# An attention and feed-forward kernel: VectorE and ScalarE in a fixed instruction order, with an explicit list for the opening

## The chip, the cores and the metric

The kernel runs on one core of a Trainium2 chip. Five engines have instruction streams of their own: TensorE (PE; its weight loads are shown apart as PEld), VectorE (DVE), ScalarE (ACT), GpSimd (POOL) and SyncE (SP, which here only issues DMAs). The metric is the device time of one execution in microseconds, lower is better.

## The reference

For four batches of 12480 tokens with 128 features: 32 learned vectors attend to the tokens, which gives `h` (32 x 128 per batch); then every token attends to `h`; the result goes through a feed-forward network (FFN) with 2048 hidden features and the ELU function.

```python
def mab(q, kv):
    s = scale * (q @ kv.transpose(0, 2, 1))
    s = s - s.max(-1, keepdims=True)
    a = np.exp(s)
    a /= a.sum(-1, keepdims=True) + 1e-09
    return a @ kv
h = mab(I, x)                 # I: the 32 vectors, for each batch
y = mab(x, h)                 # 4 x 12480 x 128
hidden = y.reshape(-1, 128) @ w_in
g = np.where(hidden > 0.0, hidden, np.exp(np.minimum(hidden, 0.0)) - 1.0)
out = g @ w_out               # 49920 x 128, float32
```

The two weight matrices arrive as 64-bit floats and are turned into 32-bit ones on the chip, from their integer halves.

## The kernel before

**Tiling.** A batch is cut into 25 blocks (15 of 512 tokens, 10 of 480), and the blocks into seven groups of two to four (`GROUPING`). `HALVES` are the pairs of blocks in a group. A *unit* (also called a pair, since it covers two chunks of 128 hidden features) is one block times one of eight pairs of chunks: 4 x 25 x 8 = 800 units, numbered n.

**The main pipeline**, one unit at a time:

- `ffn_in` (L552): two matmuls into a PSUM tile `ph`. The projection of `h` by `w_in` is multiplied directly by the attention weights, so the second attention product and the first FFN product are one matmul (L558). ACT takes the exponential, `e` (L566). There are three `ph` slots.
- `ffn_mid` (L569): DVE combines `ph` and `e` into ELU plus one (L572), into `ph` for units marked D, else into `e`.
- `ffn_split` (L576): the value is split into a high part `gh` (ACT, L581) and a low part `gl`. For D units DVE makes `gl` from `ph` (L584); for P units POOL does, in two steps (L589, L594); N units need only POOL's first step, and use plain 32-bit matmuls. `PLAN = "PDNPDPND"` gives the mark of each of a block's eight units.
- `ffn_out` (L596): matmuls (L616) of `gh`, `gl` or `e` with parts of `w_out` into an accumulator `po`, five units behind `ffn_in`; after the eighth unit DVE transposes the block (L623) and SP stores it.

**Side work.** While the FFN of batch b runs, its attention is prepared group by group (`attend`: scores L483 on PE and a DVE transpose L491; maximum L499, subtraction L500, exponential L503; sum, reciprocal and product L510 to L513; a transpose L521, a split L530 and L531, and DMAs into the six `stk` tiles L536). In the same time batch b+1 goes through its first attention (`first_half`: `load_xT` with a DMA and a DVE transpose L239, `scores` L284, `bias_of`, `weights_of` L345, `e_of` L358, `gather` L361, and the chain from `sum_es` to `stack_h` that ends in the tile `hw`). Each side step has a due time in blocks, written as a formula; the loop at L751 emits a step when its due time has come.

**What sets the order.** A planner in the framework orders each engine's instructions from its own model of their times. From the first unit on, only PE is held to the program's order (`tc.manual_schedule(engines={ET.PE})`); the transposes L239 and, after the opening, the exponentials L345 are held behind the instruction that precedes them on their engine. All other work on DVE, ACT, POOL and SP is placed by the planner. Small PSUM results of side steps use one of the two `po` slots (`bank`).

**The opening.** `first_batch` (L674) does the first half for batch 0: PE transposes of `x`, copies, scores in two phases (groups 0 to 2, then 3 to 6; `PHASES`), and the conversion of the weights in 16 pieces of 256 columns (class `Weight`, L145). The attention of block 0 alone (`attend(0, -1)`) and the projection of `h` by `w_in` end it. The planner orders all engines here.

Of the kernel before, what the change touches and what calls it, by code (L numbers as in the profile page):

```python
# [27 lines left out]
PLAN = "PDNPDPND"  # L28


@with_exitstack
def kernel(
# [47 lines left out]
    PHASES = [range(0, 3), range(3, NG)]  # L80

# [17 lines left out]

    turn = [0]  # L100

    def bank(name, take=False):
# [23 lines left out]
    ind = const.tile([M, C], F32, name="ind")  # L126
# [12 lines left out]
    WS = 256  # L139
# [5 lines left out]
    class Weight:  # L145


        def __init__(self, raw):

            self.raw = raw.rearrange("p (f two) -> p f two", two=2)  # L150

        def take_apart(self):
            lo, hi = self.raw[:, :, 0], self.raw[:, :, 1]
            part = op.tile([P, 2, WS], U32, tag="o", name="w_part")
            scale, sign = part[:, 0], part[:, 1]
            nc.vector.tensor_scalar(
                out=scale, in0=hi, scalar1=20, scalar2=0x7FF,
                op0=ALU.logical_shift_right, op1=ALU.bitwise_and,
            )
            nc.scalar.activation(sign.bitcast(F32), hi.bitcast(I32), AF.Sign)  # L160
            nc.scalar.activation(lo.bitcast(F32), lo, AF.Copy, scale=2.0**-52)
# [4 lines left out]
            nc.vector.tensor_scalar(  # L166
                out=hi, in0=hi, scalar1=0xFFFFF, scalar2=0x100000,
                op0=ALU.bitwise_and, op1=ALU.bitwise_or,
            )
            nc.gpsimd.tensor_scalar(  # L170
                out=scale, in0=scale.bitcast(F32), scalar1=-254.0, scalar2=-float(1 << 23),
                op0=ALU.add, op1=ALU.mult,
            )
            self.scale, self.low, self.top = scale.bitcast(F32), lo.bitcast(F32), hi
            self.sign = sign.bitcast(F32)

        def put_together(self, dst):
            nc.gpsimd.tensor_tensor(out=self.sign, in0=self.sign, in1=self.scale, op=ALU.mult)
            nc.vector.scalar_tensor_tensor(
                out=self.low, in0=self.top, scalar=2.0**-20, in1=self.low,  # L180
                op0=ALU.mult, op1=ALU.add,
            )
            nc.gpsimd.tensor_tensor(out=dst, in0=self.low, in1=self.sign, op=ALU.mult)
# [7 lines left out]
    def finish_w_in(s, w):  # L191
        w.put_together(win_sb[:, s * WS : (s + 1) * WS])

    WC = WS // C

    def load_w_out(quarter, pool, tag):
        n = NFC // 4
        raw = pool.tile([P, n, 2 * C], U32, tag=tag, name="w_raw")
        rows = w_out[quarter * n * P : (quarter + 1) * n * P, :]
        dma = nc.sync.dma_start(raw, rows.rearrange("(c p) d -> p c d", p=P))  # L200
        raw = raw.rearrange("p c d -> p (c d)")
        return [Weight(raw[:, i : i + 2 * WS]) for i in range(0, 2 * n * C, 2 * WS)], dma

    def finish_w_out(s, w):
        t = small.tile([P, WC, C], F32, tag="wo", name=f"wo_{s}")
        w.put_together(t.rearrange("p c d -> p (c d)"))
        for i in range(WC):
            f = s * WC + i
            if f in WHERE_N:
                nc.scalar.copy(wo_n[:, WHERE_N[f], :], t[:, i, :])  # L210
            if f in WHERE_S:
                n = WHERE_S[f]
                nc.scalar.copy(wo_h[:, n, :], t[:, i, :])
                nc.gpsimd.tensor_sub(
                    wo_l[:, n, :], t[:, i, :], wo_h[:, n, :].bitcast(F32)
                )
# [4 lines left out]
    steady = []  # L221

    def in_order(ins):
        return tc.keep_in_program_order(ins) if steady else ins

    def load_xT(b, h):
# [12 lines left out]
        tc.keep_in_program_order(nc.vector.transpose(t, xq.rearrange("p u d -> p (u d)")))  # L239
        xT[b, h] = t  # L240

    def transpose_first(b, g):
# [9 lines left out]
        for v in range(0, U, UP):  # L252
            n = min(UP, U - v)
            ps = ps_h.tile([P, 2, 512], F32, tag="ph", name=f"ps_x_{g}_{v}")
# [10 lines left out]
            for i, half in enumerate(halves):  # L265
                m = min(2, nq - 2 * i)
                copy = nc.scalar.copy if i % 2 else nc.vector.tensor_copy
# [16 lines left out]
    def scores(b, g):  # L284
# [5 lines left out]
        for j in range(nq):  # L290
# [6 lines left out]
            )  # L297

# [4 lines left out]
        )  # L303
        nc.vector.tensor_reduce(
            out=st["pm"][:np_, g : g + 1], in_=s, axis=AX.X, op=ALU.max
        )
        st["s", g] = s

    def bias_of(b, i):
        st = state[b]
        n = PHASES[i].stop
# [8 lines left out]
        nc.tensor.matmul(ps[:, : 4 * n], nsel4, apart[:, :, :n], start=True, stop=True)  # L322
        bias = small.tile([P, 1], F32, tag=f"bias{i}", name=f"bias_{b}_{i}")
        nc.vector.tensor_reduce(out=bias, in_=ps[:, : 4 * n], axis=AX.X, op=ALU.min)  # L324
        st["bias", i] = bias
        if i:
            st["scale"] = small.tile([P, 1], F32, tag="scale", name=f"scale_{b}")
            nc.scalar.activation(st["scale"], st["bias", 0], AF.Exp, bias=bias, scale=-1.0)
# [12 lines left out]
    def weights_of(b, g):  # L341
# [3 lines left out]
        in_order(nc.scalar.activation(  # L345
# [3 lines left out]
            bias=st["bias", int(g in PHASES[1])][:np_],  # L349
            scale=SCALE,  # L350
            accum_out=st["es"][:np_, g : g + 1],
        ))
# [8 lines left out]
    def gather(b, g):  # L361
        st = state[b]
        np_, U = GROUPS[g][1] * Q, GROUPS[g][2] // Q
        ps = bank(f"ps_hh_{b}_{g}")
        for u in range(U):
# [7 lines left out]
            )  # L373
        if g == 0:
            st["h"] = small.tile([P, C], F32, tag="h", name=f"h_{b}")
            nc.vector.tensor_copy(st["h"], ps[:, :C])
        elif g == PHASES[1].start:
# [420 lines left out]
```

## Time and profile before

| | |
|---|---|
| median of 3 runs | 1726.87 us (1726.18 to 1726.93) |
| the profiled execution | 1726.07 us, of it span from first to last instruction 1724.2 us |
| busy share of the span | PE 96%, DVE 89%, ACT 81%, POOL 78% |
| granted TensorE clock | mean 0.986; 0.50 from 40 to 70 us |
| first FFN matmul (L558) | at 67.6 us |
| batches 1, 2, 3 begin at | 492.4, 910.4, 1328.3 us |

A row of grouped instructions gives line, engine, operation, output and inputs with their shapes and the count, then busy microseconds and the mean in ns of one, then the engine's idle time just before them and what ended it. A row of a stretch gives its bounds and length, then busy microseconds and the number of instructions of PE, PEld, DVE, ACT and POOL, then the granted clock, the DMA share and GB/s. A row of waits gives who waited for whom, the microseconds in total, the number of times and the longest. A row of the timeline gives start, duration, engine and instruction, and in brackets the idle time before it and who ended that.

### The profile page before, as it was taken

The page shows a single profiled execution, that of the slowest core. Times are in us where ns is not written, and L with a number is a line of the kernel's source. Part 1 is how long each engine was busy: PE and PEld are TensorE (multiplying, and loading weights), DVE is VectorE, ACT ScalarE, POOL GpSimd, SP SyncE. Part 2 cuts the span into 40 slices and gives each one's busy share as a digit, 9 for nine tenths or more (in the row PEclk, how much of TensorE's full clock was granted, in tenths as well). Part 3 has the DMA queues.
Part 4 walks back from the last instruction along what each step waited for, and adds up shares of the span by engine and source line. Part 5 has one row for each costly group of instructions (what it writes and reads, how often), then busy time and mean ns, then how long its engine had stood idle before and what let it go on. Part 6 is the DMA issues. An engine that isn't in the chain of part 4 may idle for free.

```text
span 1724.2 us, 22399 instructions
## 1 busy us (share of the span) xinstructions
PE 1653.8 (96%) x7446; PEld 1174.2 (68%) x7446; DVE 1530.5 (89%) x1618; ACT 1404.2 (81%) x1643; POOL 1346.6 (78%) x970
## 2 busy tenths in 40 slices
PE   6689999999999999999999999999999999999998
PEld 4356766677676666667776676676777777777776
DVE  6889889989899998898889989888989999989986
ACT  6778888788788878888888788788878888888886
POOL 3877777778787877777778777777868888888886
PEclk9599999999999999999999999999999999999999
DMA  7363333322234233232323423411212211121111
GB/s 254 62 97 51 59 63 59 66 48 61 59 53 76 50 75 64 52 54 47 83 49 55 73 61 50 79 37 35 73 31 47 37 33 27 23 37 32 26 19 21
DMA packets 384755, 98.10 MB, mean 57 GB/s; under 512 B 364864, under 2 KB 370784, under 8 KB 384384
## 3 DMA queue, kind: packets, MB, share of 16 engines
q1 hardware_dynamic: 384640, 96.68, 29.0%
q8 instruction: 59, 0.97, 0.3%
q14 instruction: 56, 0.46, 0.1%
HBM read 48.94 MB, written 25.56 MB: 43 GB/s over the span
## 4 chain that ended last, share of the span: by engine, by line
PE 79%; DVE 10%; issue 3%; ACT 2%; DMA 1%; POOL 1%; SPq 0%; DVEq 0%; ACTq 0%; POOLq 0%
PE po L616 56%; PE ph L558 19%; DVE e L572 3%; DVE xT L239 2%; DVE gl L584 2%; ACT e L566 1%; PE ps_t L483 1%; PE ps_hh L367 1%; DVE ph L572 1%; PE ps_s L291 1%; DVE o L623 1%; DMA xq<-in_x_dram 1%; ACT gh L581 0%; ACT s L300 0%; POOL gl L594 0%
## 5 line engine op out<-in xcount | busy, mean ns | idle before, releaser
L566 ACT ACTIVATE e<-ph 128x1024 f32<-128x1024 f32 (+1 forms) x800 | 803.6, 1005 | 233.5 <-PE ph L558 227.6
L589 POOL TENSOR_SCALAR e<-e 128x1024 f32<-128x1024 f32 (+1 forms) x500 | 512.2, 1031 | 306.1 <-ACT gh L581 285.0
L594 POOL TENSOR_TENSOR gl<-e,gh 128x1024 fp32r<-128x1024 f32 (+1 forms) x300 | 704.3, 2348 | 16.6
L572 DVE SCALAR_TENSOR_TENSOR e<-ph,e 128x1024 f32<-128x1024 f32 (+1 forms) x500 | 592.6, 1188 | 78.5 <-ACT e L566 76.7
L558 PE MATMUL ph<-stk,hw 128*128 128x512 f32 (+1 forms) x1600 | 565.7, 435 | 32.5 <-DVE gl L584 14.9
L616 PE MATMUL po<-gh,wo_h 128*128 128x512 f32 (+1 forms) x1200 | 468.9, 391 | 10.4 <-ACT e L566 6.5
L616 PE MATMUL po<-gh,wo_l 128*128 128x512 f32 (+1 forms) x1200 | 465.7, 388 | 0.0
L558 PEld LDWEIGHTS ph<-stk,hw 128*128 128x128 f32 x1600 | 293.8, 190 | 209.6 <-issue 102.2
L572 DVE SCALAR_TENSOR_TENSOR ph<-ph,e 128x1024 f32<-128x1024 f32 (+1 forms) x300 | 359.3, 1198 | 59.8 <-ACT e L566 59.0
L616 PE MATMUL po<-gl,wo_h 128*128 128x512 f32 (+1 forms) x1200 | 368.4, 388 | 2.4 <-POOL gl L594 2.4
L616 PE MATMUL po<-e,wo_n 128*128 128x512 f32 (+1 forms) x800 | 367.2, 581 | 0.0
L584 DVE SCALAR_TENSOR_TENSOR gl<-ph,gh 128x1024 fp32r<-128x1024 f32 (+1 forms) x300 | 355.7, 1186 | 12.1 <-ACT gh L581 11.0
L581 ACT ACTIVATE gh<-e 128x1024 fp32r<-128x1024 f32 (+1 forms) x300 | 311.4, 1038 | 23.6 <-DVE e L572 18.5
L581 ACT ACTIVATE gh<-ph 128x1024 fp32r<-128x1024 f32 (+1 forms) x300 | 300.9, 1003 | 10.0 <-DVE ph L572 8.2
L616 PEld LDWEIGHTS po<-gh,wo_h 128*128 128x128 f32 x1200 | 226.0, 188 | 63.1 <-ACT s L300 5.7
L616 PEld LDWEIGHTS po<-gl,wo_h 128*128 128x128 f32 x1200 | 225.7, 188 | 47.7 <-POOL gl L594 3.7
L616 PEld LDWEIGHTS po<-gh,wo_l 128*128 128x128 f32 x1200 | 226.3, 189 | 45.4 <-issue 0.4
L616 PEld LDWEIGHTS po<-e,wo_n 128*128 128x128 f32 x800 | 151.0, 189 | 106.1 <-issue 91.7
L623 DVE STREAM_TRANSPOSE o<-po 128x512 f32<-128x512 f32 (+1 forms) x100 | 69.3, 693 | 12.2 <-PE po L616 12.2
L239 DVE STREAM_TRANSPOSE xT<-xq 128x1024 f32<-128x1024 f32 (+2 forms) x39 | 45.2, 1159 | 0.0
L367 PE MATMUL ps_hh<-xm,e 128*32 128x128 f32 (+2 forms) x872 | 33.3, 295 | 8.0 <-DVE bias L324 2.3
L500 POOL TENSOR_TENSOR s<-s,mx 128x512 f32<-128x512 f32 (+3 forms) x28 | 28.8, 1027 | 15.5 <-DVE mx L499 15.5
(94 smaller groups left out, 571.4 us busy)
## 6 DMA issues: line engine op xcount, KB each, us to landing
xm<-in_x_dram SPq DMA_DIRECT2D x32, 512.0 KB, 4.4
out_dram<-o SPq DMA_DIRECT2D x240, 64.0 KB, 2.0
xq<-in_x_dram SPq DMA_DIRECT2D x84, 128.0 KB, 3.6
out_dram<-o SPq DMA_DIRECT2D x160, 60.0 KB, 2.0
stk<-ahi SPq DMA_DIRECT2D x118, 64.0 KB, 2.0
xq<-in_x_dram SPq DMA_DIRECT2D x60, 120.0 KB, 3.4
stk<-ahi SPq DMA_DIRECT2D x80, 60.0 KB, 2.0
stk<-alo SPq DMA_DIRECT2D x59, 64.0 KB, 2.0
```

What stands on the lines that cost most here:

```text
L239: tc.keep_in_program_order(nc.vector.transpose(t, xq.rearrange("p u d -> p (u d)")))
L367: nc.tensor.matmul(ps[c * Q : (c + 1) * Q, :C], st["e", g][:np_, u * Q : (u + 1) * Q], st["xm", g, u - u % UP][:np_, u % UP, :], start=(u ...
L500: eng.tensor_tensor(out=s, in0=s, in1=mx.unsqueeze(2).broadcast_to([np_, U, Q]), op=ALU.subtract)
L558: nc.tensor.matmul(ph[:, i], state[b]["hw"][:, f * P : (f + 1) * P], stacks[b, k], start=True, stop=True,)
L566: nc.scalar.activation(e, ph, AF.Exp, bias=-1.0)
L572: nc.vector.scalar_tensor_tensor(out=v["g"], in0=v["ph"], scalar=1.0, in1=v["e"], op0=ALU.max, op1=ALU.min)
L581: nc.scalar.activation(v["gh"], v["g"], AF.Copy, bias=-1.0)
L584: nc.vector.scalar_tensor_tensor(out=v["gl"], in0=v["g"], scalar=-1.0, in1=v["gh"].bitcast(F32), op0=ALU.add, op1=ALU.subtract,)
L589: nc.gpsimd.tensor_scalar(out=v["e"], in0=v["e"], scalar1=-1.0, scalar2=1.0, op0=ALU.add, op1=ALU.mult)
L594: nc.gpsimd.tensor_sub(v["gl"], v["e"], v["gh"].bitcast(F32))
L616: nc.tensor.matmul(po[:, :T], w, g, start=(cp == 0 and i == 0), stop=(cp == NCP - 1 and i == len(parts) - 1),)
L623: nc.vector.transpose(o.rearrange("p u d -> p (u d)"), po[:, :T])
```

## The change

The order of DVE and ACT is fixed like that of PE: the chip gets these instructions as the program emits them.

- **Steps become generators.** A step may `yield k`: what follows is emitted k units later. `load_xT` yields 3 between the DMA and the transpose; `scores`, `gather`, `bias_of`, `share_of`, `spread_h`, `project_h` and `attend_scores` yield 1 between the matmul and what reads its result; `attend_exp` yields 3 between the subtraction on POOL and the exponential on ACT; `attend_norm` yields 3 behind the product on POOL; `ffn_out` yields 1 ahead of the transpose of the finished block. Parts of one attention group, and of one head chain (`h1` and so on), run strictly one after the other.
- **`gl` and POOL's steps** of unit n-2 are emitted in iteration n (`ffn_low`), behind the main step of n-1.
- **Due times**: scores 0.3 block later, `e_of` 0.15 block behind its exponential, block group 0 of batch 0 handled in the opening. `hw` is taken and its last rows set (`room_for_h`) ahead of the chain.
- **The opening** follows the list `FIRST` on all engines. Its names: x, y the two halves of a group's transposes, s and m scores and maximum, b bias, w exponential, e transpose, g and h gather and its sum, A to E the five parts of a weight piece, l the attention of block 0, a that of the rest of group 0, u0 to u12 the first units. It has three phases (groups 0 to 2, 3 and 4, 5 and 6). Until the list is used up, side results other than gathers use `ph` slots, and three elementwise steps of attention run on DVE, not POOL.
- **Weights** are converted in 8 pieces of 512 columns with other operations: the sign is carried by DVE's bit operations and no longer by ACT's Sign and a product on POOL; the exponent's limits are taken by POOL (max, min) for pieces 0 to 5 and by two Relu steps on ACT for 6 and 7.

The core of the diff:

```diff
+FIRST = """
+    A0 A1 B0 x0 y0 C0 B1 x1 s0 D0 y1 C1 m0 s1 D1 x2 m1 y2 x3 s2 m2 y3 b0 w0 s3 x4 w1 m3 e0
+    y4 w2 e1 x5 s4 m4 A2 g0 y5 e2 h0 g1 b1 x6 y6 w3 g2 s5 w4 h1 h2 e3 B2 s6 e4 m5 room A3 g3
+    m6 b2 B3 g4 h3 w5 w6 C2 e5 D2 sum g5 e6 h4 g6 C3 h5 share h6 D3 norm spread l0 project
+    l1 A4 stack l2 A5 l3 B4 a0 u0 a1 C4 B5 u1 a2 D4 C5 u2 E4 a3 D5 A6 u3 B6 E5 u4 C6 u5 D6
+    A7 u6 B7 E6 u7 C7 u8 D7 u9 E7 u10 u11 u12
+"""
...
     def bank(name, take=False):
+        if not steady and not take:
+            return ps_h.tile([P, 2, 512], F32, tag="ph", name=name)[:, 0]
...
-    WS = 256
+    WS = 512
...
         def take_apart(self):
+            self.part = op.tile([P, WS], U32, tag="o", name="w_part")
+            self.scale = self.part.bitcast(F32)
             nc.vector.tensor_scalar(
+                out=self.part, in0=self.hi, scalar1=20, scalar2=0x7FF,
                 op0=ALU.logical_shift_right, op1=ALU.bitwise_and,
             )
-            nc.scalar.activation(sign.bitcast(F32), hi.bitcast(I32), AF.Sign)
-            nc.scalar.activation(scale.bitcast(F32), scale, AF.Relu, bias=rebias)
-            nc.scalar.activation(
-                scale.bitcast(F32), scale.bitcast(F32), AF.Relu, bias=largest, scale=-1.0
+            nc.scalar.activation(self.low, self.lo, AF.Copy, scale=2.0**-52)
+
+        def scale_of(self, busy):
+            if busy:
+                nc.scalar.activation(self.scale, self.part, AF.Relu, bias=rebias)
+                nc.scalar.activation(self.scale, self.scale, AF.Relu, bias=largest, scale=-1.0)
+                minus, step = -254.0, -float(1 << 23)
+            else:
+                nc.gpsimd.tensor_scalar(
+                    out=self.scale, in0=self.part, scalar1=896.0, scalar2=1150.0,
+                    op0=ALU.max, op1=ALU.min,
+                )
+                minus, step = -896.0, float(1 << 23)
+            nc.gpsimd.tensor_scalar(
+                out=self.part, in0=self.scale, scalar1=minus, scalar2=step,
+                op0=ALU.add, op1=ALU.mult,
+            )
+
+        def put_together(self):
+            nc.vector.scalar_tensor_tensor(
+                out=self.part, in0=self.hi, scalar=0x80000000, in1=self.part,
+                op0=ALU.bitwise_and, op1=ALU.bitwise_or,
             )
             nc.vector.tensor_scalar(
+                out=self.hi, in0=self.hi, scalar1=0xFFFFF, scalar2=0x100000,
                 op0=ALU.bitwise_and, op1=ALU.bitwise_or,
             )
+        def finish(self, dst=None):
             nc.vector.scalar_tensor_tensor(
+                out=self.low, in0=self.hi, scalar=2.0**-20, in1=self.low,
                 op0=ALU.mult, op1=ALU.add,
             )
+            nc.gpsimd.tensor_tensor(
+                out=self.low if dst is None else dst, in0=self.low, in1=self.scale, op=ALU.mult
+            )
...
-        tc.keep_in_program_order(nc.vector.transpose(t, xq.rearrange("p u d -> p (u d)")))
+        yield 3
+        nc.vector.transpose(t, xq.rearrange("p u d -> p (u d)"))
...
     def attend_exp(b, g):
-        eng = nc.vector if lone(b, g) else nc.gpsimd
+        eng = nc.gpsimd if steady else nc.vector
         nc.vector.tensor_reduce(out=mx, in_=s, axis=AX.X, op=ALU.max)
         eng.tensor_tensor(
             out=s, in0=s, in1=mx.unsqueeze(2).broadcast_to([np_, U, Q]), op=ALU.subtract
         )
+        yield 3
         nc.scalar.activation(s, s, AF.Exp, scale=SCALE)
+        yield 1
...
-    last = first_batch(0)
-    steady.append(True)
+    with tc.manual_schedule():
+        last = first_batch(0)
     ctx.enter_context(tc.issue_after(last.ins))
     ET = mybir.EngineType
-    ctx.enter_context(tc.manual_schedule(engines={ET.PE}))
+    ctx.enter_context(tc.manual_schedule(engines={ET.PE, ET.DVE, ET.Activation}))
...
     for n, (b, k, cp) in enumerate(units):
         ffn_in(n)
-        while done <= n - min(LAG, RAMP + n // 4):
-            ffn_out(done)
-            done += 1
         if n >= 1:
             ffn_mid(n - 1)
             ffn_split(n - 1)
+        if n >= 2:
+            ffn_low(n - 2)
+        for r in list(running):
+            go_on(r, n)
+        while rest and rest[0][0] != f"u{n + 1}":
+            step = rest.pop(0)[1]
+            if step:
+                step()
+        if not rest:
+            steady.append(True)
+        while done <= n - min(LAG, RAMP + n // 4):
+            begin(n, lambda: ffn_out(done))
+            done += 1
         while side and side[0][0] <= n / NCP:
-            side.pop(0)[1]()
+            begin(n, *side.pop(0)[1:])
```

`begin` starts a step's generator and `go_on` takes it up again when its lag has passed; a step whose chain is still busy waits for its turn.

More of the change, by code (lines that the diff above doesn't have):

```diff
@@ L148, in __init__ @@
         def __init__(self, raw):
[L150 removed]
+            raw = raw.rearrange("p (f two) -> p f two", two=2)
+            self.lo, self.hi = raw[:, :, 0], raw[:, :, 1]
+            self.low = self.lo.bitcast(F32)
         def take_apart(self):
[L153 to L155 removed]
+            self.part = op.tile([P, WS], U32, tag="o", name="w_part")
@@ L306, in scores, with phases, phase_of @@
         )
-        st["s", g] = s
+    def phases(b):
+        ends = [0, 3, NG - 2, NG] if b == 0 else [0, 3, NG]
+        return [range(i, j) for i, j in zip(ends, ends[1:])]
+    def phase_of(b, g):
+        return next(i for i, groups in enumerate(phases(b)) if g in groups)
     def bias_of(b, i):
         st = state[b]
-        n = PHASES[i].stop
+        n = phases(b)[i].stop
         ps = bank(f"ps_pm_{b}_{i}")
@@ L727, in first_batch @@
-        turn[0] += 1
-        for s, w in enumerate(wout):
-            w.take_apart()
-            finish_w_out(s, w)
-        for _, step in attend(b, -1):
-            step()
-        turn[0] += 1
-        project_h(b)
-        stack_h(b)
-        return last
+        wout = [load_w_out(i, *[(xqp, "xq"), (xmp, "xm")][i // 2]) for i in range(F // WS)]
+        steps = {}
+        for g in range(NG):
+            parts = transpose_first(b, g)
+            next(parts)
+            steps[f"x{g}"] = steps[f"y{g}"] = lambda parts=parts: next(parts, None)
+            parts = scores(b, g)
+            steps[f"s{g}"] = steps[f"m{g}"] = lambda parts=parts: next(parts, None)
+            steps[f"w{g}"] = lambda g=g: weights_of(b, g)
+            steps[f"e{g}"] = lambda g=g: e_of(b, g)
+            parts = gather(b, g)
+            steps[f"g{g}"] = steps[f"h{g}"] = lambda parts=parts: next(parts, None)
@@ new lines, in first_batch @@
+        for i in range(len(phases(b))):
+            steps[f"b{i}"] = lambda i=i: list(bias_of(b, i))
+        for name, f in [
+            ("sum", sum_es), ("share", share_of), ("room", room_for_h), ("norm", norm_h),
+            ("spread", spread_h), ("project", project_h), ("stack", stack_h),
+        ]:
+            steps[name] = lambda f=f: list(f(b) or [])
+        for i, (_, f, _) in enumerate(attend(b, -1)):
+            steps[f"l{i}"] = lambda f=f: list(f() or [])
+        for i, (_, f, _) in enumerate(attend(b, 0)):
+            steps[f"a{i}"] = lambda f=f: list(f() or [])
@@ new lines, in first_batch @@
+        for s, w in enumerate(win + [w for w, _ in wout]):
+            steps[f"A{s}"], steps[f"C{s}"] = w.take_apart, w.put_together
+            steps[f"B{s}"] = lambda w=w, s=s: w.scale_of(s >= 6)
+            if s < len(win):
+                steps[f"D{s}"] = lambda w=w, s=s: w.finish(win_sb[:, s * WS : (s + 1) * WS])
+            else:
+                steps[f"D{s}"] = w.finish
+                steps[f"E{s}"] = lambda w=w, s=s: split_w_out(s - len(win), w)
+        order = FIRST.split()
+        assert sorted(n for n in order if n[0] != "u") == sorted(steps)
@@ L746 @@
         side += first_half(b) if b else []
-        for g in range(NG):
+        for g in range(b == 0, NG):
             side += attend(b, g)
@@ L750, with begin, go_on @@
     done = 0
+    running = []
+    chains = {}
+    def begin(n, step, chain=None):
+        r = [n, step, chain, None]
+        running.append(r)
+        go_on(r, n)
+    def go_on(r, n):
+        at, step, chain, parts = r
+        if parts is None:
+            if chains.setdefault(chain, r) is not r and chain:
+                return
+            parts = r[3] = iter(step() or ())
+        elif at > n:
+            return
+        lag = next(parts, None)
+        if lag is None:
+            running.remove(r)
+            if chain:
+                chains.pop(chain)
+        else:
+            r[0] = n + lag
     for n, (b, k, cp) in enumerate(units):
         ffn_in(n)
-        while done <= n - min(LAG, RAMP + n // 4):
-            ffn_out(done)
-            done += 1
         if n >= 1:
```

205 lines of the change are left out of this document (91 added, 114 removed).

## The prediction

> **What bounds the kernel now.** I read the page first, then TensorE's own waits, then busy time by stretches, then single stalls in the timeline.
>
> ```profile
> span 1724.2 us, 22399 instructions
> ...
> PE 1653.8 (96%) x7446; PEld 1174.2 (68%) x7446; DVE 1530.5 (89%) x1618; ACT 1404.2 (81%) x1643; POOL 1346.6 (78%) x970
> ```
>
> TensorE (PE) is named busy for 96% of the span and VectorE (DVE) for 89%. Both are averages, so I cut the span where its character changes: at the first FFN matmul (67.6 us), 13 units later (100.8), at the starts of batches 1, 2 and 3 (492.4, 910.4, 1328.3), inside batch 1 (766.3), and before the last block.
>
> ```profile
> core 0: us, PE busy (x) PEld busy (x) DVE busy (x) ACT busy (x) POOL busy (x), PEclk, DMA share, GB/s
> 0.00:67.60 67.60, 38.41 (x396) 24.61 (x396) 48.19 (x109) 44.24 (x112) 39.57 (x73) 0.79 0.69 199
> 67.60:100.80 33.20, 27.19 (x85) 17.04 (x85) 27.09 (x28) 24.51 (x31) 25.52 (x25) 0.77 0.33 53
> ...
> 492.40:766.30 273.90, 267.02 (x1145) 182.49 (x1143) 249.27 (x250) 223.57 (x247) 214.63 (x145) 1.00 0.36 62
> 766.30:910.40 144.10, 141.29 (x695) 105.18 (x693) 127.33 (x138) 119.25 (x142) 111.62 (x79) 1.00 0.26 57
> 910.40:1328.30 417.90, 408.05 (x1835) 287.53 (x1834) 376.57 (x388) 342.81 (x388) 326.08 (x223) 1.00 0.30 55
> 1328.30:1697.10 368.80, 368.80 (x1485) 271.51 (x1483) 333.36 (x324) 315.83 (x349) 309.67 (x211) 1.00 0.16 28
> ```
>
> Three stages can be seen. In the opening no engine is full: DVE, the busiest, works 48.2 of 67.6 us and idles 19.4. In batches 1 and 2 (418 us each) PE idles 10 us. In batch 3, which prepares no next batch, PE never idles: 24 blocks take 368.8 us. This last stretch is the floor that PE alone sets.
>
> How much of a batch's 418 us is loss? Batch 1 without its last block (14.5 us) takes 403.5, 34.7 more than the same 24 blocks of batch 3. Part of that is honest PE work, priced by single blocks (bounds are starts of a block's first FFN matmul): a plain one, one with an attention score step, one with a gather.
>
> ```profile
> 714.90:731.50 16.60, 16.60 (x94) 12.02 (x93) 14.09 (x14) 13.77 (x15) 14.05 (x10) 1.00 0.21 43
> ...
> 1407.40:1422.90 15.50, 15.50 (x63) 11.37 (x61) 13.58 (x14) 13.31 (x15) 12.61 (x9) 1.00 0.18 32
> 1438.30:1454.90 16.60, 16.60 (x69) 11.36 (x67) 14.85 (x16) 13.34 (x15) 12.89 (x10) 1.00 0.11 17
> ```
>
> Each costs 16.6 - 15.5 = 1.1 us. Batch 1 has one more attention group than batch 3's stretch, seven score groups and seven gathers, one projection, and small ones, about 0.6 together: 16 x 1.1 + 0.6 = 18 (19.8 at 1.2 each). So 34.7 - 18 to 20 leaves **15 to 16.5 us of stall per batch**, some 46 us over the three batches that prepare a next one. PE's waits after the ramp show what ends it:
>
> ```profile
> PE ph L558 <- DVE gl L584: 14.9, 12, 1.4
> PE po L616 <- ACT e L566: 6.5, 6, 1.1
> PE ph L558 <- DVE e L572: 4.4, 5, 1.4
> PE po L616 <- DVE s L491: 2.7, 4, 0.7
> ```
>
> These are 28.5 us; the rest hides inside matmuls that are counted busy. One stall, as DVE and PE saw it:
>
> ```profile
> 632.98 1.16 DVE L239 STREAM_TRANSPOSE xT<-xq 128x960 f32<-128x960 f32 x1
> 634.07 1.19 DVE L572 SCALAR_TENSOR_TENSOR ph<-ph,e 128x1024 f32<-128x1024 f32 x1
> 635.18 1.20 DVE L584 SCALAR_TENSOR_TENSOR gl<-ph,gh 128x1024 fp32r<-128x1024 f32 x1
> ...
> 636.43 0.73 PE L558 MATMUL ph<-stk,hw 128*128 128x512 f32 x2 [1.21 <-DVE gl L584]
> ```
>
> DVE did the next batch's transpose and then a main step ahead of the `gl` that would have freed a PSUM slot; PE waited 1.21 us, about that transpose. So DVE's order in the heavy part of a batch is what PE waits for. That part is nearly full of DVE work: 249.3 of 273.9 us. It holds 6.9 of the 9.7 us that PE idles in the batch, so by that share some 11 of the 15.5 us of stall; without them DVE would be busy 249.3 of 263, 95%.
>
> By PE busy time the idle to win is those 9.7 us a batch, 29 in three. [...]
>
> **The change, part by part.**
>
> *The main pipeline.* `gl` of the D pairs and POOL's steps move to the iteration after. In quiet stretches DVE already runs that order:
>
> ```profile
> 1422.88 1.23 DVE L572 SCALAR_TENSOR_TENSOR ph<-ph,e 128x1024 f32<-128x1024 f32 x1 [0.20 <-ACT e L566]
> 1425.04 1.23 DVE L572 SCALAR_TENSOR_TENSOR e<-ph,e 128x1024 f32<-128x1024 f32 x1 [0.93 <-ACT e L566]
> 1426.18 1.22 DVE L584 SCALAR_TENSOR_TENSOR gl<-ph,gh 128x1024 fp32r<-128x1024 f32 x1
> ```
>
> The main step of the next pair comes first, then `gl` of the pair before. So there it costs 0, covered by PE's 100% busy stretch; without that cover it would delay a PSUM slot by 1.2 us per D pair.
>
> *Side steps in set places.* The DVE work per batch is the same: no side instruction is added or removed. A transpose now sits three pairs behind its DMA issue, scores and gathers leave PE and come back on ACT or DVE one pair later, attention's exponential waits three pairs for POOL. One pair is 15.5/8 = 1.94 us. An iteration needs 1.2 us of DVE for the main step and 1.2 more where the pair before was D; a 1.2 us transpose in one slot puts DVE about 1 us behind (4.8 us of work in two slots of 1.94), and the next slots take it back if no second side step falls there. The old transposes fell beside an attention transpose and a score maximum in the same block; steps spread one by one are absorbed, as in the block of 1438.3, where DVE has 14.85 of 16.6 us and PE no stall. Bounds for the 46 us: all of it (every stall gone) or nothing (the same collisions, elsewhere); a loss too, since a set order can wait where the planner's would not (rival D). DVE's total load (249.3 in 273.9) leaves little room, so I take half: **7.5 us a batch, -23**.
>
> SP's queue gets the same DMAs. A load of `xq` needs its slot from the transpose two before, now three pairs later; two slots and four pairs between loads still cover it, and if they did not, DVE would stand at the transpose and every main step behind it would wait. The `hw` memset moves ahead of the head's chain, onto POOL (78% busy), at 0.
>
> *The opening.* Weights are taken apart in 8 pieces of 512 instead of 16 of 256. Rows of the first 67.6 us, then those that price the new widths:
>
> ```profile
> L179 DVE SCALAR_TENSOR_TENSOR w_raw<-w_raw 128x256 f32<-128x256 uint32 x15 | 8.0, 546 | 0.4
> L166 DVE TENSOR_SCALAR w_raw<-w_raw 128x256 uint32<-128x256 uint32 x15 | 6.4, 430 | 0.6 <-ACT w_part L160 0.2
> L156 DVE TENSOR_SCALAR w_part<-w_raw 128x256 uint32<-128x256 uint32 x15 | 5.6, 384 | 6.2 <-POOL win_sb L183 3.1 <-DMA w_raw<-in_moe_w_in_dram 2.5 <-POOL wo L183 0.6
> ```
>
> ```profile
> L572 DVE SCALAR_TENSOR_TENSOR e<-ph,e 128x1024 f32<-128x1024 f32 x300 | 363.1, 1215 | 41.3 <-ACT e L566 40.4
> L500 POOL TENSOR_TENSOR s<-s,mx 128x512 f32<-128x512 f32 x11 | 11.6, 1052 | 0.8 <-DVE mx L499 0.8
> L491 DVE STREAM_TRANSPOSE s<-ps_t 128x512 f32<-128x512 f32 x11 | 7.6, 695 | 0.0
> ```
>
> A piece of 256 costs DVE 0.546 + 0.430 + 0.384 = 1.36 us; the 15 before the first FFN matmul 20.4. A piece of 512 has two tensor_scalar (each between 0.38 and 0.86, twice the old; I take 0.5, since part of the 256-wide price is fixed) and two two-input steps (between 0.546 at 256 and 1.215 at 1024 wide: 0.75). Ahead of the first FFN matmul now stand A0 to A5, C0 to C3, D0 to D3: 6 x 0.5 + 4 x 1.25 + 4 x 0.75 = 11.0, and one transpose of attention step a0 (0.70). DVE work there: 48.2 - 20.4 + 11.0 + 0.7 = 39.5 us. With the same 19.4 us of idle the first FFN matmul comes at 58.9; with half of it (10, an estimate) at 49.5. I take 55.5: 12 us earlier. ACT loses Sign and most Relu steps, POOL the sign product; neither led, so 0.
>
> Paid back behind it: C4 to C7, D4 to D7, A6, A7 are 4 x 1.25 + 4 x 0.75 + 2 x 0.5 = 9.0, less 1.4 for the one old piece there, plus three steps of the first attention group that move from POOL to DVE (1.05 each at most, 3.2): 10.8 us more DVE work beside the first 13 units.
>
> ```profile
> 67.60:100.80 33.20, 11.79 (x27) 6.88 (x27) 0.77 0.33 53
> ```
>
> Those 13 units (two matmuls L558 each, and the first of the next at the bound) take 33.2 us and DVE idles 6.1 of them, so the cost is 4.7 (all idle filled) to 10.8 (none): I take 7. Net **-5**; bounds -13.4 (18.1 - 4.7) and +2.1 (10.8 - 8.7), beyond which nothing but new waits could push it.
>
> One price of this may be too low. The same operation and shape varies threefold:
>
> ```profile
> L156 DVE TENSOR_SCALAR w_part<-w_raw x16: 277/294/820, 6.2 to 67.6; 128x256 uint32<-128x256 uint32 x16
> ```
>
> [...]
>
> *Sum.* -23 - 5 = -28 against the profiled execution's own 1726.07 us (span 1724.2 and 1.9 around it): 1698. The median of the runs, 1726.87, stands 0.8 above that execution, so **1699**.
>
> **The rivals.**
> A, the forecast: half of the stalls go and the opening gains a little. 1685 to 1712. Chance 0.52.
> B, the side steps meet the D pairs again and only the opening gains (5, up to 13): about 1720. For it: DVE's 249 of 273.9. Chance 0.15.
> C, all stalls go and the opening gains its best: 1726.9 - 46 - 9 = 1672. For it: batch 3's 368.8 shows PE can run without idling. Against: the 95% of DVE in the heavy part. Chance 0.14.
> D, slower: ScalarE's attention exponential stands in a set place, but the subtraction it needs is still placed by the planner on POOL, where a `gl` can be ahead of it:
>
> ```profile
> L594 POOL TENSOR_TENSOR gl<-e,gh 128x1024 fp32r<-128x1024 f32 (+1 forms) x300 | 704.3, 2348 | 16.6
> L589 POOL TENSOR_SCALAR e<-e 128x1024 f32<-128x1024 f32 (+1 forms) x500 | 512.2, 1031 | 306.1 <-ACT gh L581 285.0
> ```
>
> A P pair's two steps (3.4 us) and the subtraction (1.05) are 4.4; three pairs give 5.8. With two P pairs queued (7.8) ScalarE waits 2.0 us, and behind it the next pair's exponential, then DVE and PE. At 27 groups it decides from 28/27 = 1.04 us each; at 1.7 us it gives 46 - 28 = +18: 1745. Chance 0.13.
> E, the order comes out much as the planner's and the opening's two terms cancel: 1727. For it: the quiet order above is the same already. Chance 0.06.
>
> **How the numbers follow.** 0.2%, 3.5 us, is about what a measurement of this kernel tells from no change. A, B and C are faster (0.81), E the same (0.06), D slower (0.13). The range 1674 to 1730 leaves out about half of C and nearly all of D. A's own range is 1685 to 1712.
>
> **What would show it.** Right: first FFN matmul at 52 to 59 us; 13 units later than that after 38 to 42 us; batches 1 and 2 at 408 to 413 us; the wait of L558 for `gl` halved or less; batch 3's 24 blocks at 368 to 370. Wrong: batches still at 418 (B), ScalarE's attention exponential waiting for POOL's subtraction (D), batches near 403 (C), VectorE standing at `xT` for an `xq` load.

## The result, and the profile after

The changed kernel is slower: 1750.34 us (median of 4 runs, 1747.46 to 1750.82) against 1726.53 for the kernel before on the same chip, a ratio of 1.0135 with a 95% interval of 1.0117 to 1.0152. The forecast was 1699. Medians here and below are of the runs in the chip's faster state.

The page of the changed kernel, span and busy shares:

```profile
span 1748.3 us, 22270 instructions
...
PE 1652.5 (95%) x7448; PEld 1175.6 (67%) x7448; DVE 1569.1 (90%) x1608; ACT 1384.8 (79%) x1593; POOL 1341.5 (77%) x941
```

PE has the work of before (1653.8). DVE has ten instructions fewer and 38.6 us more busy time: something on DVE became longer. The stretches, cut at the same events as in the prediction:

```profile
core 0: us, PE busy (x) PEld busy (x) DVE busy (x) ACT busy (x) POOL busy (x), PEclk, DMA share, GB/s
0.00:61.20 61.20, 39.19 (x404) 25.32 (x404) 39.42 (x85) 22.47 (x46) 28.32 (x37) 0.86 0.57 185
61.20:109.30 48.10, 29.75 (x78) 18.27 (x78) 40.99 (x42) 29.58 (x46) 32.90 (x31) 0.68 0.46 78
...
503.50:923.60 420.10, 405.77 (x1836) 287.53 (x1835) 384.57 (x388) 341.61 (x388) 325.93 (x223) 1.00 0.32 60
...
1343.80:1721.20 377.40, 368.94 (x1485) 270.13 (x1483) 343.80 (x324) 316.20 (x349) 309.39 (x211) 1.00 0.15 28
```

Three things differ. The first FFN matmul comes 6.4 us earlier. The 13 units behind it take 48.1 us instead of 33.2. And batch 3's 24 blocks, the floor in which PE did not idle before, take 377.4 instead of 368.8, with the same PE work and 10.4 us more of DVE. PE's waits name DVE's main step where they named `gl`:

```profile
PE ph L609 <- DVE e L623: 38.2, 31, 1.7
PE ps_pm L351 <- DVE apart L345: 9.1, 9, 1.2
PE po L671 <- ACT wo_h L236: 9.1, 1, 9.1
```

The main step itself kept its length (1.21 us). What stands ahead of it is the addition of EPS (the reference's 1e-09) to the sums of the attention, a step of 15 or 16 elements a row. One line's instructions, with minimum, median and maximum in ns, first of the kernel before, then of the changed one:

```profile
L511 DVE TENSOR_SCALAR sm<-sm x28: 131/310/915, 78.8 to 1624.0; 128x16 f32<-128x16 f32 x11, 128x15 f32<-128x15 f32 x8, 96x16 f32<-96x16 f32 x5, 64x15 f32<-64x15 f32 x4
```

```profile
L559 DVE TENSOR_SCALAR sm<-sm x28: 171/2104/2274, 66.2 to 1667.2; 128x16 f32<-128x16 f32 x11, 128x15 f32<-128x15 f32 x8, 96x16 f32<-96x16 f32 x5, 64x15 f32<-64x15 f32 x4
```

The same 28 steps took 11.0 us in all and now take 44.9. The timeline of the changed kernel shows one of them (start, duration):

```profile
662.88 0.61 PE L609 MATMUL ph<-stk,hw 128*128 128x512 f32 x2
663.14 2.35 POOL L649 TENSOR_TENSOR gl<-e,gh 128x1024 fp32r<-128x1024 f32 x1
663.42 2.11 DVE L559 TENSOR_SCALAR sm<-sm 96x16 f32<-96x16 f32 x1
665.56 0.25 DVE L560 RECIPROCAL sm<-sm 96x16 f32<-96x16 f32 x1
665.73 1.16 DVE L623 SCALAR_TENSOR_TENSOR e<-ph,e 128x1024 f32<-128x1024 f32 x1
...
666.94 0.50 PE L609 MATMUL ph<-stk,hw 128*128 128x512 f32 x1 [1.73 <-DVE e L623]
```

POOL's `gl` ends at 665.50, DVE's small step at 665.53: its duration stretches until POOL's step ends. Such a step is called *held* below. All 21 long ones end 25 to 36 ns behind a step of POOL, 20 of them behind `gl`; the seven that met no running POOL step, or only its end, took 171 to 175 ns. The main step behind it came 2 us late and PE stood for 1.73. In the kernel before, 15 of the 28 are lengthened, all by POOL's short step and none by `gl`. The same step there:

```profile
628.46 1.05 POOL L589 TENSOR_SCALAR e<-e 128x1024 f32<-128x1024 f32 x1 [0.63 <-ACT gh L581]
```

```profile
628.62 0.91 DVE L511 TENSOR_SCALAR sm<-sm 96x16 f32<-96x16 f32 x1
```

Why the two ends fall together the traces do not show. One kind of POOL step held nothing (last section).

### The profile page after: what moved, and what is told of

Read it like the earlier page. It is cut to its first block, busy times and chain, and to the rows that moved or that the text cites. A ratio compares the mean times of both kernels' runs of the same rounds, so it can differ in the third digit from the quotient of the medians.

```text
span 1748.3 us, 22270 instructions
## 1 busy us (share of the span) xinstructions
PE 1652.5 (95%) x7448; PEld 1175.6 (67%) x7448; DVE 1569.1 (90%) x1608; ACT 1384.8 (79%) x1593; POOL 1341.5 (77%) x941
## 4 chain that ended last, share of the span: by engine, by line
PE 74%; DVE 17%; ACT 5%; issue 2%; DMA 1%; POOL 1%; SPq 0%; DVEq 0%; ACTq 0%; POOLq 0%
PE po L671 51%; PE ph L609 18%; DVE e L623 4%; DVE ph L623 3%; ACT e L617 3%; DVE sm L559 2%; DVE gl L639 2%; PE ps_t L527 1%; PE ps_hh L399 1%; ACT gh L632 1%; PE ps_s L310 1%; DVE xT L257 1%; DVE sm L558 1%; PE ps_x L278 1%; DVE pm L327 1%
## 5 line engine op out<-in xcount | busy, mean ns | idle before, releaser
L623 DVE SCALAR_TENSOR_TENSOR ph<-ph,e 128x1024 f32<-128x1024 f32 (+1 forms) x300 | 358.9, 1196 | 62.7 <-ACT e L617 62.6
L559 DVE TENSOR_SCALAR sm<-sm 128x16 f32<-128x16 f32 (+3 forms) x28 | 44.9, 1605 | 1.0
L399 PE MATMUL ps_hh<-xm,e 128*32 128x128 f32 (+2 forms) x872 | 32.3, 285 | 2.7 <-DVE e L390 1.6
```

Source lines behind the costliest of these rows:

```text
L399: nc.tensor.matmul(ps[c * Q : (c + 1) * Q, :C], st["e", g][:np_, u * Q : (u + 1) * Q], st["xm", g, u - u % UP][:np_, u % UP, :], start=(u ...
L559: nc.vector.tensor_scalar_add(sm, sm, EPS)
L623: nc.vector.scalar_tensor_tensor(out=v["g"], in0=v["ph"], scalar=1.0, in1=v["e"], op0=ALU.max, op1=ALU.min)
```

## The experiments

Theories: T1, the hold beside POOL at its new place is the loss; T2, a fixed order makes instructions wait at a queue's head; T3, the opening's list pushes weight work behind the first FFN matmul. One table first, from the traces: the first FFN matmul, the time to the first matmul of unit 13, from there to batch 3's last block ("rest"), and the median. From the last block to the end all take 27.0 or 27.1 us.

| kernel | first | 13 units | rest | median |
|---|---|---|---|---|
| before | 67.6 | 33.2 | 1596.3 | 1726.5 |
| changed | 61.2 | 48.1 | 1611.9 | 1750.3 |
| e1 no EPS | 61.1 | 46.8 | 1572.3 | 1709.1 |
| e2 before, no EPS | 67.5 | 36.7 | 1598.8 | 1732.2 |
| e3 EPS one unit later | 60.9 | 47.6 | 1595.8 | 1733.2 |
| e5 EPS strided | 60.7 | 47.6 | 1620.9 | 1758.5 |
| e6 no EPS, planned from u0 | 62.5 | 39.5 | 1586.3 | 1716.2 |
| e7 no EPS, pieces ahead | 60.1 | 45.6 | 1572.8 | 1707.5 |
| e8 no EPS, old opening | 68.2 | 32.3 | 1577.9 | 1706.9 |
| e9 no EPS, planned opening | 73.5 | 28.6 | 1572.3 | 1703.5 |
| e10 two reciprocals for EPS | 61.1 | 47.6 | 1581.8 | 1720.0 |
| e11 EPS, planned from u0 | 62.8 | 40.1 | 1605.4 | 1735.8 |
| e12 no EPS, planned 13 units | 62.6 | 38.5 | 1574.0 | 1702.3 |
| e13 e9 and three edits | 73.3 | 26.6 | 1582.9 | 1712.0 |
| e14 EPS one unit earlier | 60.6 | 47.4 | 1594.3 | 1731.6 |
| e15 EPS two units earlier | 61.1 | 47.9 | 1598.2 | 1736.0 |
| e16 e14, planned 13 units | 62.9 | 39.9 | 1594.4 | 1725.8 |

**e1: the held step taken out.**

```diff
-        nc.vector.tensor_scalar_add(sm, sm, EPS)
```

> The changed kernel without the addition of EPS in the attention of the tokens (L559). The sum of a row holds exp(0) = 1, so that adding 1e-9 leaves the float32 as it is. Theory T1 (the set order puts this small VectorE step always beside POOL's 2.35 us gl, and it is held until that ends: 28 x 1.6 us = 44.9 us of VectorE, and a stall of TensorE of some 2 us each time): the 28 steps cost TensorE 28 x 1 to 2 us, so 20 to 35 us go: 1715 to 1730 us; batch 3's 24 blocks back at 367 to 370 us from 377.4, batches 1 and 2 at 408 to 415 from 420. Theory T2 (the loss is of the set order itself, instructions held behind waits at the head of a queue; the long step only absorbs a wait that then shows at the next instruction): the reciprocal or its neighbour takes over the wait, under 5 us go: 1745 to 1750. Theory T3 (the loss is the opening, where weight pieces stand behind the first units): under 5 us go too, and the start of batch 1 stays at 503.

Measured 1709.09 us, ratio to before 0.990 (0.9884 to 0.9917): 41 us less than the changed kernel. The same place in its timeline:

```profile
650.01 0.61 PE L608 MATMUL ph<-stk,hw 128*128 128x512 f32 x2
...
650.28 2.39 POOL L648 TENSOR_TENSOR gl<-e,gh 128x1024 fp32r<-128x1024 f32 x1
...
650.55 0.25 DVE L559 RECIPROCAL sm<-sm 96x16 f32<-96x16 f32 x1
650.72 1.16 DVE L622 SCALAR_TENSOR_TENSOR e<-ph,e 128x1024 f32<-128x1024 f32 x1
...
651.93 0.88 PE L608 MATMUL ph<-stk,hw 128*128 128x512 f32 x2
```

The reciprocal runs in 0.25 us while POOL's `gl` runs: it is not held. PE's next unit starts after 1.92 us instead of 4.06. Batch 1 is where the prediction had put it (408 to 413), and batch 3's 24 blocks, which held no stall before, are slightly below their 368 to 370:

```profile
492.90:903.10 410.20, 403.76 (x1837) 288.09 (x1835) 374.17 (x381) 341.38 (x388) 325.72 (x223) 1.00 0.33 61
...
1313.30:1680.20 366.90, 366.90 (x1484) 270.88 (x1483) 332.55 (x318) 316.06 (x348) 309.27 (x211) 1.00 0.16 28
```

T1's direction holds, but the 41 us are more than its 20 to 35, and the total lies below its band; T2 and T3 do not explain 41 us.

**e2: the same line out of the kernel before.**

> The kernel before without the same addition (L511), as a control. There it took 392 ns in the mean (131 to 915), 11 us in all. T1: the planner's order seldom put it beside POOL's gl, so 0 to 7 us go (1720 to 1727). If the step itself, not its place, were what costs, the gain would be as large as in the changed kernel (20 us and more). T2 and T3: 0 to 3 us.

1732.15 us, ratio 1.0033 (1.0021 to 1.0045): slower by 5.5, where all theories expected zero or a small gain. The planner, with one step less, orders other steps anew (13 units 3.5 us longer, batch 1 418.6 instead of 418.0). So taking the step out is no gain in every order, and a planner's order moves by some us when a step goes; what the step's 11.0 us are worth there is hidden by that.

**e3: normalization one unit later, e5: the same step with a stride.**

```diff
 def attend_norm(b, g):   # e3
+        if steady:
+            yield 1
```

> The changed kernel with attend_norm's first part (maximum's sum, EPS, reciprocal, POOL's product) emitted one unit later in the steady part, where POOL's own work of the iteration is that of a D unit (none). The addition of EPS stays. T1: beside an idle POOL, or one in a step that lets VectorE through, L559 takes 0.15 to 0.5 us instead of 1.6 in the mean, and 15 to 30 us go (1720 to 1735). If POOL's queue still runs the gl of unit 0 one unit later, L559 stays over 1 us and the time at 1745 to 1755. T2: the place in the order matters little, 1745 to 1755. T3: the same.

```diff
-        sm = small.tile([P, U], F32, ...)[:np_]   # e5
+        sm = small.tile([P, U, 2], F32, ...)[:np_, :, 0]
```

> The changed kernel with the sums of attend_norm kept at every second element (a tile of U x 2, of which element 0 is used), so that the addition of EPS has the same place, the same count of elements and the same neighbours, and reads and writes with a stride. [...] If a strided step is held too, L559 stays at 1.6 us and the time at 1745 to 1752. T2: no change, 1745 to 1752, with the wait showing at the neighbour.

e3:

```profile
L561 DVE TENSOR_SCALAR sm<-sm x28: 166/694/1241, 65.9 to 1653.9; 128x16 f32<-128x16 f32 x11, 128x15 f32<-128x15 f32 x8, 96x16 f32<-96x16 f32 x5, 64x15 f32<-64x15 f32 x4
```

e5:

```profile
L559 DVE TENSOR_SCALAR sm<-sm 128x16 f32<-128x16 f32 (+3 forms) x28 | 44.9, 1605 | 1.0
```

One unit later the step takes 15.1 us in all instead of 44.9 (0.54 in the mean, just above the 0.5 expected, and 1.24 at the longest), and the kernel takes 1733.2, 17 us less, inside T1's band. With a stride the step is as long as before (1605 ns in the mean in both, 2276 and 2274 at the longest). e5 takes 8 us more than the changed kernel; the step does not account for them (44.9 us in both), and the cause is open (last section).

**e6: DVE and ACT planned from u0, no EPS. e11: the same with EPS.**

```diff
-    ctx.enter_context(tc.manual_schedule(engines={ET.PE, ET.DVE, ET.Activation}))
+    ctx.enter_context(tc.manual_schedule(engines={ET.PE}))
```

> The kernel without EPS in the attention, with VectorE and ScalarE left to the planner again from the first unit on (only TensorE held to the program's order, as in the kernel before); the steps in parts, the due times, the lag of gl and the opening's list stay. It stands beside the same kernel with the set order, 1709.1 us, batches 1 and 2 at 410.2 us. If the set order itself brings the 8 us a batch, they go back to 415 to 420 us and the time to 1725 to 1740. If the steps' parts and due times bring it, whoever orders the engines, they stay at 409 to 412 and the time at 1705 to 1713.

> The changed kernel with EPS in the attention, VectorE and ScalarE left to the planner from the first unit on. It completes a table of two by two: set order with EPS 1750.3, without 1709.1; planned order without 1716.2. T1 (the loss comes from a fixed order that puts the step beside POOL's gl every time): the planner's places vary, L559 takes 0.3 to 0.8 us in the mean, and the time is 1713 to 1725, far below the set order's. Rival (the step costs wherever it stands, and the order has no part in it): L559 over 1.3 us and 1740 to 1760.

e6 took 1716.2 us, between its two cases: batches 415.3 and 412.6. Of the 24.0 us that e1 gains in the rest against the kernel before, all else that differs (the steps in parts, the due times, the lag of `gl`, the work that the opening takes over, EPS) brings 10.0 together, the set order 14.0 more. e11 took 1735.8, between T1's band and the rival's:

```profile
L559 DVE TENSOR_SCALAR sm<-sm x28: 154/1132/1933, 74.3 to 1635.4; 128x16 f32<-128x16 f32 x11, 128x15 f32<-128x15 f32 x8, 96x16 f32<-96x16 f32 x5, 64x15 f32<-64x15 f32 x4
```

The planner too lets the step grow (1.14 us in the mean, 0.15 at the shortest, 1.93 at the longest). So T1 has to be mended: it is not the fixed order alone that brings the step to such a place, since the rest of the change does it too; the set order makes the step longer (1.60 us in the mean against 1.14). EPS costs the rest 19.1 us under the planner (1605.4 against 1586.3) and 39.6 in the set order (1611.9 against 1572.3). With EPS kept, the set order of the regular part is therefore 6.5 us worse than the planner's in these traces; without EPS it is 14.0 better.

**e7, e8, e9, e12: the opening, all without EPS.** e7 moves `C4 B5 D4 C5 E4 D5 A6 B6 E5` of the list ahead of `u0`. e8 takes the opening of the kernel before and sets the order from unit 8. e9 drops `with tc.manual_schedule()` around the opening and sets DVE's and ACT's order from unit 12; e12 keeps the list up to u0 and lets the planner order DVE and ACT in units 0 to 12:

```diff
+    ctx.enter_context(tc.manual_schedule(engines={ET.PE}))   # e9, e12
...
         if not rest:
+            if not steady:
+                ctx.enter_context(tc.manual_schedule(engines={ET.PE, ET.DVE, ET.Activation}))
             steady.append(True)
```

> The kernel without EPS in the attention (1709.1 us; first FFN matmul at 61.1, the first matmul of unit 13 at 108.0), with pieces 4 and 5 of w_out finished ahead of u0 in the list. Theory R1 (the opening loses its time because the first output matmuls wait for these pieces: unit 3 lasts 13.9 us, TensorE waits 8.4 us for wo_h): the first FFN matmul moves to 66 to 71, unit 3 falls to 2 to 4 us, unit 13 comes at 102 to 106 and the time falls by 2 to 6 us, to 1703 to 1707. Theory R2 (the stretch is bound by VectorE, 41 of 47 us busy there, part of it steps held beside POOL, and a step moved ahead is only paid at another place): unit 13 at 107 to 110, 1708 to 1712.

> The kernel without EPS in the attention, with the opening of the kernel before (16 pieces of 256 columns, ordered by the planner up to unit 8), and the set order from unit 8 on. If the new opening is what costs 7 us (unit 13 at 108.0 against 100.8 before), the first FFN matmul is at 67 to 68, unit 13 at 100 to 103, batch 1 starts at 484 to 488 against 492.9, and the time is 1700 to 1705. If what the new opening does ahead (group 0 of the attention of batch 0, on VectorE) has to be paid here after unit 13, batch 1 starts at 490 to 494 and the time is 1706 to 1712.

> The kernel without EPS in the attention, with the planner ordering all engines in the opening and VectorE and ScalarE up to unit 12 (TensorE keeps the program's order from the first unit on, as before); the steps are emitted as in the list, the weights converted with the new operations in 8 pieces, and the order is set from unit 12 on. If the list's order is what costs (a step at a queue's head that waits), unit 13 comes at 99 to 104 and the time is 1700 to 1706. If the operations cost (VectorE's weight steps held beside POOL, 41 us of VectorE in the first 13 units), unit 13 stays at 106 to 112 and the time at 1707 to 1714.

> The kernel without EPS in the attention (1709.1 us; unit 13 at 107.9), with the list ordering the opening up to u0, the planner ordering VectorE and ScalarE in units 0 to 12, and the set order from there on. In the run with a planned steady part unit 13 came at 102.1. If the list's order of the first 13 units is what loses the opening's gain: first FFN matmul at 61 to 63, unit 13 at 101 to 103, batches at 410, and 1702 to 1705 us. If the planner's gain there is only work put off to later units: batch 1 starts at 491 to 493 and the time is 1707 to 1710.

e7: 1707.5, not told apart from e1 (0.9894, 0.9879 to 0.9909) and between the two bands. The stall of unit 3 fell from 13.9 to 7.6 us, but units 1 and 2 grew by 4.3 and 1.0: PE's 8.4 us of waiting for `wo_h` are gone, and 4.1 for a transpose on DVE have come in. e8: 1706.9; its opening is as quick as expected (unit 13 at 100.5, batch 1 at 485.7), but the rest is 5.6 us longer than e1's, so the total lies in the band of the other reading. e9: 1703.5, unit 13 at 102.1: as expected if the list's order costs. Its first FFN matmul is the latest of all, at 73.5, and its 13 units the second shortest: an early first matmul is worth nothing by itself here. e12: 1702.33, ratio 0.9857 (0.9841 to 0.9873), the fastest kernel here, beside e9:

```profile
0.00:62.60 62.60, 38.69 (x404) 25.33 (x404) 40.28 (x87) 23.61 (x48) 28.94 (x37) 0.85 0.55 181
62.60:101.10 38.50, 27.32 (x79) 17.25 (x79) 36.22 (x39) 28.27 (x44) 32.87 (x31) 0.70 0.62 101
101.10:486.30 385.20, 378.82 (x1732) 270.94 (x1729) 349.56 (x360) 320.09 (x365) 303.77 (x210) 1.00 0.32 62
```

So with the list's operations unchanged, its order of the first 13 units costs 46.8 - 38.5 = 8.3 us there, and 6.8 in the whole time (1709.1 - 1702.3). With EPS it is much the same: 47.4 in e14, 39.9 in e16.

**e10: two steps that are not held, at the same place.** `nc.vector.reciprocal(sm, sm)` stands three times in e1 in place of once.

> The kernel without EPS in the attention (1709.1 us), with two further reciprocals at the place where EPS was added: 1/x is taken three times, which gives 1/x again but for rounding. Each takes 0.25 us and is not held beside POOL, so VectorE gets 14 us of small steps at the disputed place without a hold. T1 (the hold is what costs, not the place or one step more): steps of 0.25 us, the time at 1709 to 1716. Rival (any added work of VectorE at this place stops TensorE; the run with the step one unit later left 15 us there and still lost 24): 1720 to 1735.

```profile
L559 DVE RECIPROCAL sm<-sm x28: 243/252/253, 66.1 to 1638.4; 128x16 f32<-128x16 f32 x11, 128x15 f32<-128x15 f32 x8, 96x16 f32<-96x16 f32 x5, 64x15 f32<-64x15 f32 x4
```

None is held, yet the kernel takes 1720.0: 9.5 us more in the rest for 14 us of DVE time. This is the lower edge of the rival's band and above T1's, so the rival is partly right: DVE has so little room at this place that a step which is not held costs PE about 0.7 us for each us. The held step costs about 0.9 (39.6 us for 44.9). By this count the hold costs mainly because it makes a step of 0.17 us one of 1.6 in the mean.

**e13: an attempt at a still faster version.** On e9, EPS also out of `share_of`, and in `bias_of` the matmul one unit behind `apart`, with later due times.

> A version meant to beat all: opening and units 0 to 12 ordered by the planner, the set order from there on, no EPS in the attention, none in the sum of the first attention either (its total holds exp(0) = 1 as well; the reciprocal reads PSUM directly, where TensorE waited 5.4 us for it in three places), and in bias_of the matmul one unit behind VectorE's product apart (6.1 us of waits, the product held beside POOL for 1.64 us three times), with the exponentials 0.15 block later. Without the last three edits it took 1703.5. If these waits are TensorE's end to end, 6 to 9 us go: 1695 to 1698. If they only move to the next step: 1701 to 1705.

1712.0, above both expected bands and slower than e9: the waits moved. PE's 5.4 us of waiting for `r` in e9 are gone, but of these two waits the first was 2.8 us there and the second 8.6:

```profile
PE po L671 <- DVE bias L356: 10.1, 3, 3.4
PE ps_pm L353 <- DVE apart L344: 7.3, 5, 4.1
```

**e14, e15, e16: the place alone, EPS kept.**

```diff
+        early = [0, 0, 0.125, 0]   # e15: 0.25
-        return [(b * NBLK + at + gap * i, ...
+        return [(b * NBLK + at + gap * i - early[i], ...
```

> The changed kernel with attend_norm due 0.125 block (one unit) earlier; EPS and all work stay. In the changed kernel L559 is held by POOL's gl of unit 3; one unit earlier POOL has the short step of unit 2 (1.05 us) or nothing. If the hold is what costs, about 0.9 us of TensorE for each us of it: L559 at 0.2 to 0.8 us in the mean, 5 to 22 us of VectorE, and 1712 to 1730 us. If another property of the order costs, L559 falls and the time stays at 1735 to 1750.

> The same, two units earlier, where POOL runs the gl of unit 0 (2.35 us) and the step meets its second half or more. If the hold is what costs: L559 at 0.7 to 2.0 us in the mean, and 1725 to 1750 us, above the run with one unit. If the time follows anything else, it is at 1712 to 1720 with L559 held, or at 1735 and more without.

> EPS kept and attend_norm one unit earlier, the list ordering the opening up to u0, the planner VectorE and ScalarE in units 0 to 12, and the set order from there on. The planned ramp brought 6.8 us to the kernel without EPS. If it adds to the moved step: 5 to 8 us below the run with attend_norm one unit earlier, 1705 to 1724 us, that is faster than before with all of the work kept. If the two interfere, within 3 us of that run.

In e15 the first group of batches 1 to 3 is normalized ahead of its exponential, so that group's output is another one. The step in e14:

```profile
L559 DVE TENSOR_SCALAR sm<-sm 128x16 f32<-128x16 f32 (+3 forms) x28 | 21.3, 760 | 1.0
```

and in e15:

```profile
L559 DVE TENSOR_SCALAR sm<-sm 128x16 f32<-128x16 f32 (+3 forms) x28 | 33.0, 1179 | 1.0
```

The rest of the program by DVE time in the disputed steps: none 1572.3, 14 us not held 1581.8, 15.1 (e3) 1595.8, 21.3 (e14) 1594.3, 33.0 (e15) 1598.2, 44.9 (changed) 1611.9. The ends of this row follow the hold, its middle hardly: e3 and e14 lose 23.5 and 22.0 us for 15 and 21 us of step, more than its length, and e14's 1731.6 lies just outside its band. e15 is inside its own. Moving the part also moves the sum, the reciprocal and POOL's product; what share they have is open. e16, with all of the work kept, takes 1725.8, 5.8 below e14 as expected, just outside the expected 1705 to 1724, and the same as before (ratio 0.9994, 0.9984 to 1.0003). No version here with EPS beats the kernel before.

## Why the prediction was wrong, point by point

- **Side steps, -23.** By the table the rest went from 1596.3 to 1611.9: +15.6. The step that failed is the sentence under this term that the DVE work per batch is the same because no side instruction is added or removed. It counted instructions, not their lengths beside POOL: the 28 steps grew by 34 us, and with them out (e1) the rest is 39.6 us shorter. Without the held step the direction that the prediction argued for comes out, at -24.0. That this is so close to -23 is in part luck: half of the stalls was a choice between all and nothing, e1 has one kind of step less than the forecast kernel, and not all of the 24.0 is stall (batch 3's 24 blocks, where PE never idled, went from 368.8 to 366.9).
- **Steps that grow beside POOL.** The prediction doubted one price by the spread of its row, that of the weight steps in the opening (L156), and looked at no spread in the steady part. The trace of the kernel before had the rows for it: POOL 78% busy, and L511 at 131 to 915 ns for 15 or 16 elements a row. Such a spread, sixfold (154 to 915) within the one form 96x16, was the sign.
- **First FFN matmul, 55.5.** Came at 61.2. The DVE work ahead of it was right (39.5 forecast, 39.42 measured). The idle was not: 21.8 us, more than the 19.4 of before and not the 16 taken. Less work did not shorten the chain; DVE waited 6.2 us for PE's transposes there, 2.9 before:

```profile
DVE xT L287 <- PE ps_x L278: 6.2, 5, 2.9
```

- **Paid back behind it, +7 (4.7 to 10.8).** It was +14.9. DVE's work there grew by 13.9 us (27.1 to 41.0) and not by 10.8, and its idle was not filled (6.1 before, 7.1 now). Its weight steps in these 13 units were priced at 9.0 us and took 15.0:

```profile
L196 DVE SCALAR_TENSOR_TENSOR w_part<-w_raw,w_part 128x512 uint32<-128x512 uint32 x4 | 4.9, 1217 | 3.0 <-POOL w_part L190 3.0
L206 DVE SCALAR_TENSOR_TENSOR w_raw<-w_raw 128x512 f32<-128x512 uint32 x4 | 4.1, 1020 | 0.0
L172 DVE TENSOR_SCALAR w_part<-w_raw 128x512 uint32<-128x512 uint32 x2 | 3.0, 1501 | 0.0
L200 DVE TENSOR_SCALAR w_raw<-w_raw 128x512 uint32<-128x512 uint32 x4 | 3.0, 744 | 0.1
```

  Beside no POOL step they are 0.68, 0.67, 0.41 and 0.43 us, near the 0.75 and 0.5 assumed; L196 is 2.82 us at its longest, beside `gl`. The term also priced the late pieces as DVE work alone. PE stood for the split weights themselves, 9.1 us for `wo_h` (shown above) and

```profile
PE po L671 <- POOL wo_l L237: 4.2, 1, 4.2
```

  In the kernel before PE had neither wait in its 13 units. With the planner's order of these units (e12) both are gone, and the payback is 38.5 - 33.2 = 5.3 us, inside the forecast's bounds. How the 14.9 divide between longer DVE steps and late weights is open: e7, which took the wait for `wo_h` away, gained only 1.2 us in these units.
- **Pipeline and SP, 0.** No sign against either: PE's wait for `gl`, 14.9 us before, is gone from its list, and DVE stands nowhere for `xq`.
- **Rivals.** D gave the right sign and nearly the time (1745) by a mechanism that did not occur: ScalarE has no wait for POOL's subtraction. Its chance of 0.13 was the whole for slower, and the actual mechanism, longer steps on DVE by meeting POOL, was no rival for the steady part at all. C's sum takes 9 us for the opening's best, where the prediction's own bound is 13.4; nothing here hangs on it.

The sum, against before: opening -6.4 + 14.9, rest -24.0 + 39.6, together +24.1, which is the difference of the two spans (1748.3 - 1724.2).

## What to carry to other kernels

When a change moves steps on DVE, ask for each kind what POOL runs at its new place, and read the spread of one form in one line. Here a step of 15 or 16 elements a row took 0.15 us in one place and 0.92 in another, and the upper end showed which POOL step it met: 0.92 beside the short step of 1.05 us, 2.27 beside the `gl` of 2.36. The held step cost up to that length on DVE, and with DVE busy 90% of the span, PE paid most of it (39.6 us for 44.9). A step that rounds away (EPS beside a sum of at least 1) can be left out, but try it in the order that is used: it gave 41 us in the set order and lost 5.5 in the kernel before. An explicit order for a crowded opening can lose to a planner while an explicit order in the regular part wins (here only without EPS): set them apart and test each alone.

## What the runs showed of the hardware

- In the changed kernel a two-input step on DVE was lengthened as well: `apart` (12 to 28 elements a row) took 1.64 us beside `gl` three times and 0.17 to 0.19 us beside no POOL step. A tensor_reduce of 480 or 512 elements a row (0.63 to 0.69 us beside `gl`, 0.61 to 0.69 beside no POOL step), the reciprocal of the sums (0.25; 0.24 to 0.25) and the main steps with one input in PSUM (1.12 to 1.23; 1.15 to 1.22) were not.
- Not every POOL step lengthened what ran beside it. The one EPS step that is not among the 28, for the attention of block 0, ran inside a POOL step of the weights in the changed kernel and was not lengthened:

```profile
56.30 1.92 POOL L185 TENSOR_SCALAR w_part<-w_part 128x512 f32<-128x512 uint32 x1 [5.47 <-DVE w_part L172]
```

```profile
57.21 0.18 DVE L559 TENSOR_SCALAR sm_-1_662<-sm_-1_662 128x16 f32<-128x16 f32 x1
```

  The two-input `apart` beside this kind of step took 0.16 and 0.19 us there, as long as beside none. Why it held nothing is open.
- Longer matmuls in e5, not explained: e5 only doubled one small tile. Its rows for one group of matmuls against the changed kernel's:

```profile
L671 PE MATMUL po<-gh,wo_h 128*128 128x512 f32 x720 | 283.3, 393 | 9.7 <-ACT wo_h L236 9.1 <-DVE s L537 0.6
```

```profile
L671 PE MATMUL po<-gh,wo_h 128*128 128x512 f32 x720 | 287.5, 399 | 9.2 <-ACT wo_h L236 8.6 <-DVE s L537 0.6
```

  PE was busy 408.8 us of batch 1 instead of 405.8 for the same matmuls. No run tested the cause.
